# Block-diagonal queries times keys laid 64 per block of 32 queries, in a fused windowed-attention and feed-forward kernel

## The chip, the cores and the metric

The kernel runs on one NeuronCore of a Trainium2 chip. Its five engines are named here as in the profile: PE is TensorE (matrix products; PEld its weight loads), DVE is VectorE, ACT is ScalarE, POOL is GpSimd, and SP is SyncE, which here issues the DMAs. The metric is the time of one execution on the device, in microseconds (us); lower is better. A run before and after the change is compared by medians.

## What is computed

The reference is attention with fixed windows, followed by a normalised two-layer feed-forward with a residual. Cut to what matters:

```python
B, H, S, D = 8, 8, 576, 64
window, dilation = 32, 4
scores = q @ k.T / 8                      # per batch and head
rel = pos[:, None] - pos[None, :]
plain = (rel >= 0) & (rel < 32)                         # heads 0 to 3
dil   = (rel >= 0) & (rel < 128) & (rel % 4 == 0)       # heads 4 to 7
attn = softmax(where(mask, scores, -1e9))
x = (attn @ v), heads side by side        # (8, 576, 512)
xn = (x - mean) / sqrt(var + 1e-6) * g
out = x + relu(xn @ w_ch1) @ w_ch2        # 512 -> 2048 -> 512
```

Each query has at most 32 keys. In a plain head these are the last 32 positions; in a dilated head they are every fourth of the last 128. The host orders the dilated heads' positions by residue modulo 4 within each tile of 128, so that in both kinds of head a block of 32 queries needs just two blocks of 32 keys: its own and one before it, 64 scores a query.

## The kernel before

The 4608 rows are cut into 36 tiles of 128 positions, nine to each pair of sequences of 576, and the tiles into 12 blocks of three. A tile goes through loading (`load_tile_now`), preparation (`attn_prep`), scores, softmax (`attn_softmax`), values (`attn_values`), normalisation (`norm`) and a transposing DMA; a block then goes through the feed-forward (`ffn`: 16 up products' groups at L490, then down products at L513). All products are made in half precision from operands split into a high and a low half, with three products for each (high x high, low x high, high x low). The low half of an up product's result, `hl`, is made on VectorE at L497 from PSUM; the PSUM buffer `ps_z` comes free after it. There are two such buffers.

The weights come as 64-bit floats. During the first part of the run, chunk by chunk (32 of them), they are loaded into `w_raw` (five buffers, `RAWS`), brought to float32 by ScalarE (L548, L550), VectorE (L552, L553), TensorE (sums, L560) and GpSimd (L569), and split into halves (`split`, L141 to L149).

Queries and keys are prepared in two layouts. The first five tiles (`PACKED`) hold the plain heads in the lower 64 partitions and the dilated ones in the upper 64 (`prep_packed`); `Q_DVE` puts the queries' low half on VectorE in tiles 1 and 4 instead of on GpSimd. From tile 5 on (`prep_stacked`) queries stand with their high half in the lower partitions and their low half in the upper ones (L268, L269), and keys are loaded twice, once for each half of the partitions (L172, L173); tile 5 itself also rebuilds the keys of tile 4 in the new layout (L280, L281). The last 32 keys of the tile before are copied in front by GpSimd (L245).

Scores are made in two ways as well. In the first five tiles (`attn_scores_apart`) each block of 32 queries has products of its own, 64 rows by 32 columns of TensorE, and the scores come out compact: two mask additions of 128x256 on VectorE (L352). From tile 5 on (`attn_scores`) a head's 128 queries are multiplied by 160 keys (plain) or by 128 keys of this tile and 128 of the one before (dilated), and VectorE picks from PSUM, with the mask added, what each block of 32 queries needs: four additions of 32 partitions x 256 for the plain heads (L311) and four for the dilated ones (L325). Both kinds go through one PSUM tile, `ps_s`, of two banks.

The order of the work is written out: each step is a unit with a time, either by rules (pace, gaps) or, for most steps of the first tiles, from the table `TIMES`; units are emitted in order of these times, and a scheduler with a model of the engines orders the instructions of each engine from there, with L496 and L497 at high priority. Each engine then works in its order and waits on semaphores.

Of the kernel before, what the change touches and what calls it, by code (L numbers as in the profile page):

```python
# [7 lines left out]
F16 = mybir.dt.float16  # L8
# [8 lines left out]
P = 128  # L17
H = 8
# [12 lines left out]
NQK = 2 * HP * P  # L31
NBLK = NT // NB
PACKED = 5
EARLY = 5
# [8 lines left out]
Q_DVE = (1, 4, 5)  # L43
CW, RAWS = 1, 5
# [3 lines left out]
TAIL_POOL = 1  # L48
# [4 lines left out]
# Steps of the start that the rules of the plan would place elsewhere, and where they go.  # L53
# [3 lines left out]
# Powers of two that the norms of the scaled operands stay under: of the columns of w1 and w2 (L1),  # L57
# and of v (L2).
# [6 lines left out]
def attention_then_ffn(ctx: ExitStack, tc, qkv, masks, g, w1, w2, out):  # L65
# [23 lines left out]
    vh_b = [const.tile([P, H, D + 1], F16, name=f"vh{i}") for i in range(NV)]  # L89
    for i in range(NPT):  # L90
        nc.gpsimd.memset(pt_a[i], 0.0)
        nc.gpsimd.memset(pt_d[i], 0.0)
# [5 lines left out]
    # A quarter of w1's columns is at its number as halves (high, low), and before that one further as  # L98
    # float32; the last place then is free.
# [8 lines left out]
    # Chunk f is at f as halves (high, low), and before that as float32 four further, the last four  # L108
    # in the last place of w1.
# [55 lines left out]
    def load_tile_now(t):  # L165
        qk32 = work.tile([P, 2, 2, HP, P], F32, name="qk32", bufs=1)
        v32 = work.tile([P, H, D], F32, name="v32", bufs=1)
        if t < PACKED:
            nc.sync.dma_start(out=qk32[:, 0], in_=qkv[t, :, 0:NQK])
        else:  # L170
            src = qkv[t, :, 0:NQK].rearrange("(a d) e -> d a e", a=2)
            for on in (slice(0, D), slice(D, P)):  # L172
                nc.sync.dma_start(out=qk32[on].rearrange("d a x h c -> d a (x h c)"), in_=src)  # L173
        state["load", t] = nc.sync.dma_start(out=v32, in_=qkv[t, :, NQK:]).ins
        state[t] = dict(q32=qk32[:, :, 0], k32=qk32[:, :, 1], v32=v32)
# [29 lines left out]
    def stack_v(t):  # L205
        """The last values that plain heads of the next tile use, for products with (high, high, low)."""
# [6 lines left out]
    def rescale_v(t):  # L213
        """Brings tile t's values, split, to the scale of the next tile's, which is no larger."""
# [7 lines left out]
    def attn_prep(t):  # L222
        st = state[t]
        if t < PACKED:
            prep_packed(t)
        else:
            prep_stacked(t)
# [8 lines left out]
    def halves_of(x32, hi, lo, on_dve=False):  # L236
        nc.scalar.copy(hi, x32)  # L237
        (nc.vector if on_dve else nc.gpsimd).tensor_tensor(out=lo, in0=x32, in1=hi, op=ALU.subtract)  # L238

    def keys_before(t, old, new):  # L240
        """The last keys of the tile before."""
        if t % TPP == 0:
            nc.gpsimd.memset(new[:, :, 0:W], 0.0)
        else:
            (nc.gpsimd if TAIL_POOL else nc.vector).tensor_copy(new[:, :, 0:W], old[:, :, P : P + W])  # L245

    def prep_packed(t):
        """The first half of the heads in the lower half of the partitions, the second in the upper."""
# [542 lines left out]
```

## Time and profile before

| | us |
|---|---|
| median of three runs | 1007.41 |
| lowest and highest run | 1006.25, 1008.2 |
| span of the profiled execution, first to last instruction | 1002.2 |
| median less span: what lies around the instructions | 5.2 |
| busy in the span: TensorE, VectorE, GpSimd, ScalarE | 905.7, 666.6, 386.7, 336.9 |
| mean granted TensorE clock, as a share of full speed | 0.985 |

The profile comes from an execution of its own, and its span leaves out what precedes the first instruction and follows the last; the table puts the median beside it. A row of the groups' view names the line, the engine, the operation, what is written and read, the shapes and the count; then come the total busy time, the mean in nanoseconds, and the idle time of the engine just before, with what ended it. A row of the timeline begins with start and length in microseconds, and in brackets stands the idle time ahead of it and its releaser. A matmul's length includes its way through the array, so several are in flight at a time and only differences of starts tell what one costs in a row of them.

### The profile page before, as it was taken

What the parts mean: (1) busy time and instruction counts of PE and PEld (TensorE: products, weight loads), DVE (VectorE), ACT (ScalarE), POOL (GpSimd) and SP (SyncE); (2) the same over time, 40 slices, a digit from 0 to 9 for tenths busy, and PEclk for the clock granted to TensorE, in tenths of its full rate; (3) what the DMA queues carried; (4) which work ended last, traced back from release to release, by engine and by line L of the source; (5) the groups of instructions that cost most, each with busy time, mean ns of one, the idle gap of its engine ahead of it and who ended that gap; (6) DMA issues with size and microseconds to landing.
All of it is one profiled execution on the core that took longest, in us unless ns stands there. A gap on an engine that the chain in (4) does not pass through costs nothing.

```text
span 1002.2 us, 18434 instructions
## 1 busy us (share of the span) xinstructions
PE 905.7 (90%) x7396; PEld 537.7 (54%) x7396; DVE 666.6 (67%) x1458; ACT 336.9 (34%) x601; POOL 386.7 (39%) x371
## 2 busy tenths in 40 slices
PE   3255789999999989999999989999999999999998
PEld 2244765554555545555555545555555555565553
DVE  6999997694567476576667576586676576576111
ACT  6775673341222342233222242233232232221110
POOL 6777776361332342343342342343342342311000
PEclk9996899999999999999999999999999999999999
DMA  7565845333323553334423542343423333101000
GB/s 250 172 211 173 224 129 131 85 73 72 95 54 78 137 107 76 88 64 76 99 54 77 139 107 66 94 68 76 100 53 77 87 65 78 44 12 27 27 1 32
DMA packets 76742, 92.13 MB, mean 92 GB/s; under 512 B 48240, under 2 KB 50416, under 8 KB 76656
## 3 DMA queue, kind: packets, MB, share of 16 engines
q1 hardware_dynamic: 76656, 90.95, 37.9%
q8 instruction: 58, 0.95, 0.4%
q14 instruction: 28, 0.23, 0.1%
HBM read 70.45 MB, written 9.44 MB: 80 GB/s over the span
## 4 chain that ended last, share of the span: by engine, by line
PE 54%; DVE 24%; POOL 8%; DMA 5%; issue 4%; ACT 4%; SPq 1%; POOLq 0%; ACTq 0%; DVEq 0%
PE ps_o L513 27%; PE ps_z L490 20%; DVE pt_d L382 5%; PE ps_v L424 4%; DMA qk<-in_qkv 4%; POOL qs L269 3%; PE ps_s L293 2%; DVE hl L497 2%; DVE pt_a L376 2%; DVE w_sb L553 2%; DVE pt_a L378 2%; DVE sc L311 2%; DVE xn L456 1%; POOL sc L364 1%; POOL pk L371 1%
## 5 line engine op out<-in xcount | busy, mean ns | idle before, releaser
L513 PE MATMUL ps_o<-w_sb,hh 128*128 128x512 f16 x1152 | 339.3, 380 | 3.1 <-DVE w_sb L149 1.7
L490 PEld LDWEIGHTS <-w_sb 128*128 128x128 f16 x2688 | 241.2, 100 | 159.6 <-issue 17.2
L490 PE MATMUL ps_z<-xT,w_sb 128*128 128x384 f16 (+1 forms) x1536 | 211.6, 293 | 12.6 <-DVE hl L497 12.5
L490 PE MATMUL ps_z<-w_sb 128*128 128x384 f16 x1152 | 202.7, 326 | 9.4 <-DVE hl L497 9.3
L513 PE MATMUL ps_o<-w_sb,hl 128*128 128x512 f16 x576 | 210.8, 380 | 0.0
L497 DVE SCALAR_TENSOR_TENSOR hl<-ps_z,hh 128x384 f16<-128x384 f32 (+1 forms) x188 | 105.2, 562 | 110.8 <-ACT hh L496 107.9
L513 PEld LDWEIGHTS <-hh 128*128 128x128 f16 x1152 | 110.9, 98 | 125.3 <-issue 3.0
L496 ACT ACTIVATE hh<-ps_z 128x384 f16<-128x384 f32 (+1 forms) x188 | 92.2, 493 | 245.0 <-PE ps_z L490 244.9
L382 DVE STREAM_TRANSPOSE pt_d<-pk 32x256 f32<-32x256 f32 x144 | 90.9, 631 | 2.5
L238 POOL TENSOR_TENSOR kld<-qk,khd 128x512 f16<-128x512 f32 x31 | 35.9, 1158 | 141.4 <-ACT khd L237 140.0
L513 PEld LDWEIGHTS <-hl 128*128 128x128 f16 x576 | 56.5, 98 | 62.2 <-issue 2.5
L447 POOL TENSOR_TENSOR rstd<-rstd,mhalf 128x1 f32<-128x1 f32 x36 | 21.2, 589 | 170.6 <-DVE rstd L446 169.2
L269 POOL TENSOR_TENSOR qs<-qk,qs 64x1024 f16<-64x1024 f32 x31 | 66.0, 2129 | 32.4 <-ACT qs L268 30.6
L293 PEld LDWEIGHTS <-qs 64*32 64x32 f16 (+1 forms) x1464 | 60.9, 98 | 27.3 <-ACT khp L237 6.2
L311 DVE TENSOR_TENSOR sc<-ps_s,mask_sb 32x256 f32<-32x256 f32 x124 | 52.0, 419 | 29.9 <-PE ps_s L293 28.4
L238 POOL TENSOR_TENSOR klp<-qk,khp 128x512 f16<-128x512 f32 x36 | 42.9, 1193 | 69.8 <-ACT khp L237 61.2
L519 DVE SCALAR_TENSOR_TENSOR row<-ps_o,s,x 128x512 f32<-128x512 f32 x36 | 26.9, 749 | 62.1 <-PE ps_o L513 61.2
L462 POOL TENSOR_TENSOR xl<-xn,xh 128x512 f16<-128x512 f32 x36 | 43.1, 1198 | 43.2 <-ACT xh L461 43.1
L569 POOL TENSOR_TENSOR w_sb<-w_sb,w_raw 128x512 f32<-128x512 f32 x32 | 47.9, 1511 | 27.9 <-PE ps_o L560 12.5
L325 DVE TENSOR_TENSOR sc<-ps_s,mask_sb 32x256 f32<-32x256 f32 x124 | 52.0, 419 | 6.1 <-PE ps_s L293 4.2
L424 PE MATMUL ps_v<-vh,pt_a 128*128 128x65 f16 x288 | 38.5, 202 | 17.8 <-DVE pt_a L378 17.3
L148 ACT ACTIVATE vh<-v,sv 128x512 f16<-128x512 f32 x34 | 24.5, 721 | 89.5 <-PE ps_v L424 72.7
(97 smaller groups left out, 1100.6 us busy)
## 6 DMA issues: line engine op xcount, KB each, us to landing
qk<-in_qkv SPq DMA_DIRECT2D x67, 512.0 KB, 6.6
w_raw<-in_w SPq DMA_DIRECT2D x32, 512.0 KB, 4.7
v<-in_qkv SPq DMA_DIRECT2D x36, 256.0 KB, 3.0
out_x<-row SPq DMA_DIRECT2D x36, 256.0 KB, 2.0
row<-in_qkv SPq DMA_DIRECT2D x34, 256.0 KB, 3.6
v_b<-vh SPq DMA_DIRECT2D x64, 16.2 KB, 1.8
v_b<-vl SPq DMA_DIRECT2D x32, 16.0 KB, 2.0
xT<-xh SPq DMA_TRANSPOSE x18, 5.2
```

What stands on the lines that cost most here:

```text
L238: (nc.vector if on_dve else nc.gpsimd).tensor_tensor(out=lo, in0=x32, in1=hi, op=ALU.subtract)
L269: nc.gpsimd.tensor_tensor(out=qsv[D:P], in0=st["q32"][D:P], in1=qsv[D:P], op=ALU.subtract)
L293: nc.tensor.matmul(out, lhs, rhs, start=(n == 0), stop=(n == len(terms) - 1))
L311: nc.vector.tensor_tensor(out=sc[pj, 0:HP, :], in0=ps[pj, :, W * j : W * j + 2 * W], in1=mask_sb[pj, m : m + 1, :].broadcast_to([W, HP, 2 ...
L325: nc.vector.tensor_tensor(out=sc[pj, HP:H, :].rearrange("p h (t i) -> p h t i", t=2), in0=ps[pj].rearrange("p h (t c) -> p h t c", t=2)[:, ...
L382: nc.vector.transpose(dd[pj].rearrange("p t h (i r) -> p r t h i", r=DIL)[:, j], pk[pj, HP:H, :].rearrange("p h (t i) -> p t h i", t=2),)
L424: nc.tensor.matmul(oo, l, r, start=(n == 0), stop=(n == len(mm) - 1))
L490: nc.tensor.matmul(z[:, n], l, r, start=(m == 0), stop=(m == len(mm) - 1))
L496: nc.scalar.activation(hh, z, AF.Relu)
L497: nc.vector.scalar_tensor_tensor(out=hl, in0=z, scalar=0.0, in1=hh, op0=ALU.max, op1=ALU.subtract)
L513: nc.tensor.matmul(o, l, r, start=(f == 0 and m == 0), stop=(f == NFC - 1 and m == 2))
L569: nc.gpsimd.tensor_tensor(out=dst, in0=dst, in1=hi, op=ALU.mult)
```

## The change

There is one layout and one way of making scores for all tiles. The queries' tiles `q_b` (high and low, two of each) are cleared once and hold, for each half of a tile and each head, a 128x128 stationary operand: the lower 64 partitions have the dimensions of the first 32 queries, the upper 64 those of the next 32, each at its own columns, and the rest stays zero. The keys are laid beside it as 64 columns: in the lower partitions the 64 keys of the first block of queries, in the upper partitions those of the second. One product thus gives two blocks of compact scores, and two products (for the two halves of the tile) fill the 128 rows. The plain heads' keys are placed by the loads, with the last 32 keys of the tile before read again from memory; the dilated heads' keys of the tile before are copied on VectorE from its `kd`.

The scores of all heads fill one PSUM bank (`ps_s` has two buffers of one bank each now). They are masked in one addition of 128x512, or in two of 128x256 where plain and dilated heads need different masks (first, fifth and sixth tile of nine). In the softmax the separate float32 tile `p32` is gone: the high half is written first and the exponentials then replace the scores, of which there is one buffer instead of two. The raw weights have four buffers instead of five. `PACKED`, `EARLY`, `Q_DVE` and `TAIL_POOL` are gone; `TIMES` is as it was.

```diff
-CW, RAWS = 1, 5
+CW, RAWS = 1, 4
...
-    ps_s = ctx.enter_context(tc.tile_pool(name="ps_s", bufs=1, space=PSUM))
+    ps_s = ctx.enter_context(tc.tile_pool(name="ps_s", bufs=2, space=PSUM))
...
+    NQB = 2
+    q_b = [[const.tile([P, 2 * QPITCH], F16, name=f"q_{x}{i}") for x in "hl"] for i in range(NQB)]
+    for x in (x for pair in q_b for x in pair):
+        nc.gpsimd.memset(x.bitcast(F32), 0.0)
...
     def load_tile_now(t):
-        qk32 = work.tile([P, 2, 2, HP, P], F32, name="qk32", bufs=1)
+        q32 = work.tile([P, H, P], F32, name="q32", bufs=1)
+        k32 = work.tile([P, H * P + W], F32, name="k32", bufs=1)
         v32 = work.tile([P, H, D], F32, name="v32", bufs=1)
...
+        if t % TPP:
+            old = qkv[t - 1, 0:D, HP * P : NQK].rearrange("d (h c) -> d h c", h=HP)
+            nc.sync.dma_start(out=kv[lo, 0:HP, 0:W], in_=old[:, :, 3 * W : P])
+        nc.sync.dma_start(out=kv[lo, 0:HP, W:P], in_=keys[:, :, 0 : 3 * W])
+        nc.sync.dma_start(out=k32[lo, HP * P + W :], in_=qkv[t, D:P, HP * P : NQK])
+        nc.sync.dma_start(out=k32[hi, 0 : H * P].rearrange("d (a e) -> d a e", a=2), in_=src[1])
+        for on in (lo, hi):
+            nc.sync.dma_start(out=q32[on].rearrange("d (a h) c -> d a (h c)", a=2), in_=src[0])
...
+    def prep_qk(t):
+        st = state[t]
+        qh, ql = q_b[t % NQB]
+        q32 = st["q32"].rearrange("p h (b c) -> p b h c", b=2)
+        for a in range(2):
+            on, cols = slice(D * a, D * (a + 1)), slice(W * a, W * (a + 1))
...
+            nc.scalar.copy(at[0][:, :, :, cols], q32[on, :, :, cols])
+            nc.gpsimd.tensor_tensor(
+                out=at[1][:, :, :, cols], in0=q32[on, :, :, cols], in1=at[0][:, :, :, cols], op=ALU.subtract
+            )
+        kp = work.tile([P, 2, HP, P], F16, name="kp")
+        kd = work.tile([P, 2, HP, 2, 2, W], F16, name="kd", bufs=2)
...
+            nc.vector.tensor_copy(
+                kd[:, :, :, :, 0].rearrange("p x h b i -> p (x h) b i"),
+                state[t - 1]["kd"][:, :, :, :, 1].rearrange("p x h b i -> p (x h) b i"),
+            )
+        for (hi, lo), src in (
+            ((kp[:, 0], kp[:, 1]), k32[:, 0:HP]),
+            ((kd[:, 0, :, :, 1], kd[:, 1, :, :, 1]), k32[:, HP:H].rearrange("p h (b c) -> p h b c", b=2)[:, :, :, W:]),
+        ):
+            nc.scalar.copy(hi, src)
+            nc.gpsimd.tensor_tensor(out=lo, in0=src, in1=hi, op=ALU.subtract)
...
     def attn_scores(t):
...
+        ps = ps_s.tile([P, H, 2 * W], F32, name="ps_s")
+        for h in range(H):
+            mm = [(x[:, (b * H + h) * P : (b * H + h + 1) * P], y[2 * h + b]) for b in range(2) for x, y in st["terms"]]
+            for n, (l, r) in enumerate(mm):
+                nc.tensor.matmul(ps[:, h], l, r, start=(n == 0), stop=(n == len(mm) - 1))
+        sc = work.tile([P, H, 2 * W], F32, name="sc", bufs=1)
+        plain, dil = {0: 1, 4: 2}.get(tp, 0), {0: 3, 4: 4, 5: 5}.get(tp, 0)
+        for hs, m in ((slice(0, H), 0),) if plain == dil else ((slice(0, HP), plain), (slice(HP, H), dil)):
             nc.vector.tensor_tensor(
-                out=sc[pj, 0:HP, :],
-                in0=ps[pj, :, W * j : W * j + 2 * W],
...
+                out=sc[:, hs], in0=ps[:, hs],
+                in1=mask_sb[:, m : m + 1, :].broadcast_to([P, hs.stop - hs.start, 2 * W]), op=ALU.add,
             )
...
-        p32 = work.tile([P, H, 2 * W], F32, name="p32", bufs=1)
...
-        nc.scalar.activation(p32, sm, AF.Exp, scale=sc_qk)
         nc.scalar.activation(pk16[:, :, :, 0], sm, AF.Exp, scale=sc_qk)
-        nc.gpsimd.tensor_tensor(out=pk16[:, :, :, 1], in0=p32, in1=pk16[:, :, :, 0], op=ALU.subtract)
+        nc.scalar.activation(sm, sm, AF.Exp, scale=sc_qk)
+        nc.gpsimd.tensor_tensor(out=pk16[:, :, :, 1], in0=sm, in1=pk16[:, :, :, 0], op=ALU.subtract)
```

More of the change, by code (lines that the diff above doesn't have):

```diff
@@ L301, in attn_scores @@
+        st["terms"] = ((qh, kw[0]), (ql, kw[0]), (qh, kw[1]))
     def attn_scores(t):
@@ L303, in attn_scores @@
         tp = t % TPP
-        sc = work.tile([P, H, 2 * W], F32, name="sc")
-        ps = ps_s.tile([P, HP, 256], F32, name="ps_s")
-        for h in range(HP):
-            products(ps[:, h, 0 : W + P], [(x[:, h], y[:, h]) for x, y in st["plain"]])
-        m = {0: 1, 4: 2}.get(tp, 0)
-        for j in range(4):
-            pj = slice(W * j, W * (j + 1))
-            nc.vector.tensor_tensor(
-                out=sc[pj, 0:HP, :],
-                in0=ps[pj, :, W * j : W * j + 2 * W],
-                in1=mask_sb[pj, m : m + 1, :].broadcast_to([W, HP, 2 * W]),
-                op=ALU.add,
-            )
```

125 lines of the change are left out of this document (21 added, 104 removed).

## The prediction, made before the result was known

> **What bounds the kernel now.** I began with the page's head and its busy shares, then a table of three stretches by windows.
>
> ```profile
> span 1002.2 us, 18434 instructions
> PE 905.7 (90%) x7396; PEld 537.7 (54%) x7396; DVE 666.6 (67%) x1458; ACT 336.9 (34%) x601; POOL 386.7 (39%) x371
> ```
> ```profile
> 0.00:125.00 125.00, 59.73 (x1325) 52.24 (x1326) 113.58 (x217) 80.36 (x145) 89.56 (x85) 0.90 0.69 206
> 125.00:150.00 25.00, 22.71 (x239) 15.79 (x238) 24.06 (x50) 17.84 (x28) 18.16 (x13) 0.97 0.49 130
> 175.00:950.00 775.00, 753.12 (x5376) 431.69 (x5374) 502.54 (x1134) 223.94 (x406) 262.01 (x263) 1.00 0.35 76
> ```
>
> The columns are the stretch, its length, the busy time of PE, PEld, DVE, ACT and POOL, the granted clock, the DMA share and GB/s. Two kernels sit in one. In the first 125 us TensorE works 60 us, while VectorE works 114 and GpSimd 90: here the weights are converted and split, and VectorE sets the pace (24.06 of 25 us still in the next window). From 175 us on TensorE works 753 of 775 us: there a change is worth something only if it takes work from TensorE or ends one of its waits. So I asked next what TensorE waits for from 175 us to the end (microseconds in total, times, longest).
>
> ```profile
> PE ps_z L490 <- DVE hl L497: 15.9, 18, 1.5
> PE ps_v L424 <- DVE pt_a L378: 3.0, 6, 1.5
> ```
>
> Nearly all of it is VectorE being late with hl, the low half of an up product's result, which frees the PSUM buffer for the next product. 15.9 + 3.0 = 18.9 us is the most that a shorter VectorE queue can give back in that part. Then I looked at what stood in VectorE's queue ahead of a late hl; the timelines of both engines show it, here for the first and the last of five such places (at 372, 446, 598, 672 and 821 us).
>
> ```profile
> 370.00 1.72 DVE L311 TENSOR_TENSOR sc<-ps_s,mask_sb 32x256 f32<-32x256 f32 x4
> ...
> 818.28 1.72 DVE L311 TENSOR_TENSOR sc<-ps_s,mask_sb 32x256 f32<-32x256 f32 x4
> ```
> ```profile
> 372.36 0.32 PE L490 MATMUL ps_z<-w_sb 128*128 128x384 f16 x1 [1.48 <-DVE hl L497]
> ...
> 820.65 0.66 PE L490 MATMUL ps_z<-w_sb 128*128 128x384 f16 x3 [1.51 <-DVE hl L497]
> ```
>
> Four mask additions (L311), which the change removes, occupy VectorE for 1.72 us, and TensorE stands 1.5 us for the hl that had to queue behind them.
>
> **TensorE's own work.** The scores of a tile now take 48 products of 128x128 by 64 columns (8 heads, 2 halves of the tile, 3 terms), instead of 8 of 160 and 16 of 128 columns from tile 5 on, and instead of 144 of 64x32 in the first five tiles. A busy matmul time includes the pipeline, so I take starts.
>
> ```profile
> 401.82 0.19 PE L424 MATMUL ps_v<-vl,pt_d 128*128 128x64 f16 x1
> ...
> 402.09 0.19 PE L424 MATMUL ps_v<-vl,pt_d 128*128 128x64 f16 x1
> ...
> 408.41 0.23 PE L293 MATMUL ps_s<-khp,qs 128*128 128x160 f16 x1
> ...
> 408.96 0.59 PE L513 MATMUL ps_o<-w_sb,hh 128*128 128x512 f16 x2
> ...
> 414.47 0.22 PE L293 MATMUL ps_s<-khd,qs 128*128 128x128 f16 x1
> ...
> 415.36 3.74 PE L490 MATMUL ps_z<-xT,w_sb 128*128 128x384 f16 x22
> ```
> ```profile
> 109.82 0.23 PE L293 MATMUL ps_s<-khp,qs 64*32 64x64 f16 x6
> 109.88 0.19 PE L293 MATMUL ps_s<-klp,qs 64*32 64x64 f16 x3
> 109.90 0.23 PE L293 MATMUL ps_s<-khp,qs 64*32 64x64 f16 x6
> ```
>
> Products of the values have just the new shape: nine start in 402.09 - 401.82 = 0.27 us, 30 ns each. 48 of them are 1.44 us. The old ones: eight in 0.55 us and sixteen in 0.89, together 1.44. In the early tiles nine small ones start in 0.08 us, so 144 take 1.3 us. TensorE gains and loses nothing: the zero blocks of the queries cost no time, because the columns streamed stay about the same. The bound on the other side is the weight load, one per product.
>
> ```profile
> L293 PEld LDWEIGHTS <-qs 128*128 128x128 f16 x744 | 51.5, 98 | 15.6 <-DVE sc L311 1.4
> ```
>
> Were none of its 98 ns hidden, 48 - 24 = 24 more loads would cost 2.35 us a tile, 73 us over 31 tiles. I take zero, since the nine products above had a load each and started 30 ns apart. The Trainium skill, "TensorE: Matmul & The Clock Gate", section "LDWEIGHTS (loading the stationary operand)", gives a load columns / 1.2 ns, whatever the rows, some 107 ns here; paid in series that would add 24 x 107 ns x 31, an estimate of 80 us. By that rule the change fails; the trace agrees with the duration, 98 ns, and not with paying it in series.
>
> **VectorE and GpSimd, per tile.**
>
> ```profile
> L311 DVE TENSOR_TENSOR sc<-ps_s,mask_sb 32x256 f32<-32x256 f32 x124 | 52.0, 419 | 29.9 <-PE ps_s L293 28.4
> L325 DVE TENSOR_TENSOR sc<-ps_s,mask_sb 32x256 f32<-32x256 f32 x124 | 52.0, 419 | 6.1 <-PE ps_s L293 4.2
> ...
> L553 DVE SCALAR_TENSOR_TENSOR w_sb<-w_raw,w_sb 128x512 int32<-128x512 int32 x32 | 31.1, 985 | 0.2
> ...
> L433 DVE TENSOR_TENSOR x<-ps_v,rs 128x512 f32<-128x512 f32 x36 | 24.8, 688 | 0.8
> ...
> L552 DVE TENSOR_SCALAR w_sb<-w_sb 128x512 int32<-128x512 int32 x32 | 22.6, 719 | 1.8 <-ACT w_sb L548 1.4
> ...
> L352 DVE TENSOR_TENSOR sc<-ps_s,mask_sb 128x256 f32<-128x256 f32 x10 | 3.7, 410 | 0.0
> ...
> L238 DVE TENSOR_TENSOR qs<-qk,qs 128x512 f16<-128x512 f32 x2 | 2.5, 1227 | 0.0
> ...
> L281 DVE COPY kld<-klp 64x512 f16<-64x512 f16 x2 | 0.8, 388 | 0.1
> ```
> ```profile
> L269 POOL TENSOR_TENSOR qs<-qk,qs 64x1024 f16<-64x1024 f32 x31 | 66.0, 2129 | 32.4 <-ACT qs L268 30.6
> ...
> L238 POOL TENSOR_TENSOR kld<-qk,khd 128x512 f16<-128x512 f32 x31 | 35.9, 1158 | 141.4 <-ACT khd L237 140.0
> ...
> L245 POOL COPY khp<-khp 128x128 f16<-128x128 f16 x31 | 11.6, 374 | 11.5 <-PE ps_s L293 11.2
> ...
> L92 POOL MEMSET pt_d<- 128x1024 f32 x1 | 1.0, 955 | 0.0
> ```
>
> From tile 5 on eight additions of 419 ns (3.35 us) become one of 128x512 out of PSUM, for which L433 is the nearest row, 0.69; three tiles in nine need two masks, two of 0.41. Added is a VectorE copy of the old keys of the dilated heads (512 halves, nearest row L281, 0.39). Net 3.35 - 0.69 - 0.39 = 2.3 us less a tile. Two waits are new on VectorE, with hl queued behind them: the key copy waits for GpSimd's low keys of the tile before, and the additions for GpSimd's last pass over the same scores buffer, now a single one. Both end a tile earlier, so I cost them at nothing; where tiles crowd together, one GpSimd pass, 1.16, is the other end. GpSimd: the queries' low half is two of 64x512, half of L269 each, 2.13 together as before; the keys' second half shrinks from 1.16 to 0.58, and two copies of some 0.37 go: 1.3 us less. In the first five tiles it is the other way: q low was one 128x512 of 1.16 and becomes 2.13, and 0.58 is added for the dilated keys. Tiles 1 and 4 had q low on VectorE (L238, 1.23 each), which moves to GpSimd. For tiles 1 to 4 GpSimd thus gets 2 x 0.97 + 2 x 2.13 + 4 x 0.58 - 8 x 0.37 = 5.5 us more. It also clears the four query tiles once: 1088 words each, by the row below some 4 x 1.0 us, over before the conversions that VectorE begins at 9.27 us (a row further down), so I cost it at nothing, and at its 4 us if that cover fails. ScalarE gets about the same work, and at 80 of 125 us it has room.
>
> **Stretch to 125 us.** The first tile's load is six DMAs in SP's queue instead of two, ahead of the weights.
>
> ```profile
> 1.20 0.42 SPq L169 DMA_DIRECT2D qk<-in_qkv  x1
> ...
> 2.61 2.44 SPq L544 DMA_DIRECT2D w_raw<-in_w  x5
> ```
> ```profile
> 9.27 0.43 DVE L552 TENSOR_SCALAR w_sb<-w_sb 128x512 int32<-128x512 int32 x1 [1.40 <-ACT w_sb L548]
> 9.73 0.69 DVE L553 SCALAR_TENSOR_TENSOR w_sb<-w_raw,w_sb 128x512 int32<-128x512 int32 x1
> ```
> ```profile
> ACT w_sb L548 <- DMA w_raw<-in_w: 12.4, 9, 3.1
> ```
>
> Four more issues at 0.42 to 0.49 are 1.9 us, and VectorE's conversions, which wait for the first weights until 9.27, shift by it. Tiles 0 to 4 load 1 MB of queries and keys instead of 0.5: at the window's 206 GB/s 2.5 us of transfer each, and only four instead of five raw weight buffers run ahead. Queued behind these loads on SP are the weight loads, and ScalarE waits for those 12.4 us already, so nothing to 5 x 2.5 = 12.5 comes to light; I take 2.5, as VectorE's backlog covers most. GpSimd slows VectorE: alone L552 takes 0.43 and L553 0.69, on average 0.72 and 0.98; 32 x (0.29 + 0.29) = 18.6 us for GpSimd's 89.6, 0.21 each, so 5.5 us more cost 1.2. On VectorE itself: -2.5 (q low), +1.6 (four key copies; if each first waits out a GpSimd subtraction of 1.16, 6.2), -0.4 (additions of tiles 1 to 3, 0.82 to 0.69). Sum: 1.9 + 2.5 + 1.2 - 1.3 = +4.3. The Trainium skill, "SBUF — State Buffer", section "SBUF: two separate sides", says that VectorE (two SBUF inputs, or a two-port mode) and GpSimd hold a shared port pair in turn for a whole instruction; taken fully, those 5.5 us would cost 5.5, and the total be 4.3 us higher. L552's stretched mean agrees in kind, but 0.21 in size argues for 1.2.
>
> **Stretch 125 to 175 us.** Tile 5's eight additions become two (-2.5), its special transition from one key layout to the other goes (the two copies of 388 ns alone -0.8, smaller ones uncosted), one key copy comes (+0.4), and GpSimd has 1.3 us less in each of three tiles. VectorE is full there, so I count -2.9 in full and half of GpSimd's 3.9: -4.8.
>
> **From 175 us on.** At the five places 1.72 us of additions become 0.69: 5 x 1.03 = 5.2. Of the other 9 us of waiting for hl, most behind transposes that stay, I take a third, 3, since all of VectorE's queue is 2.3 us shorter a tile. -8.2, between 0 (the waits form again behind the transposes) and -18.9.
>
> Sum: 4.3 - 4.8 - 8.2 = -8.7. The profiled span is 1002.2; the median of the three runs is 1007.41, 5.2 more for what lies around the span, and that stays. 1007.4 - 8.7 = 998.7.
>
> **Rivals.** *The start loses more than the rest gains.* The weights become late: the five larger loads show in full (12.5 instead of 2.5) and each key copy waits out a subtraction (6.2 instead of 1.6), so the first stretch costs 18.9, against 13.0 gained later: +5.9, 1013.3. It decides from a start that loses over 13.0 us. For it: ScalarE's 12.4 us. Against: VectorE is busy 114 of 125, so loads are seldom the last to come. *Waits form anew:* hl waits behind transposes instead, the start's terms cancel: 1007. *More than forecast:* most of the 18.9 goes and the start is neutral: 1007.4 - 15 - 4.8 = 987.6. *Weight loads in series:* +73 - 8.7, 1072; the 30 ns speak against it.
>
> **The numbers.** Forecast 0.50 (its own range 992 to 1005), more than forecast 0.15, no change 0.10, slow start 0.22, loads in series 0.03. About 0.2%, 2 us, is what a measurement of this kernel can tell. Faster 0.65, same 0.10, slower 0.25; the range 986 to 1015 leaves out the loads in series and the tails of both sides.
>
> **What would show it.** L311 and L325 gone, one or two additions near 0.69 in all a tile; score products 30 ns apart; TensorE's wait for hl from 175 us on down from 15.9 to some 8; the first conversion near 11 us and the last weight's conversion some 4 us later than now. Wrong if the score products start over 50 ns apart, if the hl waits stay near 16, or if the last conversion comes over 13 us later.

## The result, and the profile after

The changed kernel takes 1031.01 us, the median of four runs (1028.36 to 1033.89), beside 1006.87 for the kernel before (four runs): a ratio of 1.0236, 95% interval 1.0214 to 1.0258, or 24.1 us more. The forecast was 998.7, its range ended at 1015, and slower had a chance of 0.25. The direction was wrong, and the size lies outside the range.

The head of the page after, with the busy shares, and then the windows that the prediction read (stretch, length, busy time of PE, PEld, DVE, ACT and POOL with instructions, granted clock, DMA share, GB/s):

```profile
span 1032.1 us, 19046 instructions
PE 912.2 (88%) x7660; PEld 543.6 (53%) x7660; DVE 596.6 (58%) x1270; ACT 348.9 (34%) x642; POOL 374.7 (36%) x356
```
```profile
0.00:125.00 125.00, 46.66 (x593) 40.81 (x594) 107.84 (x193) 74.43 (x133) 92.71 (x85) 0.89 0.67 196
125.00:150.00 25.00, 22.06 (x410) 21.39 (x408) 23.04 (x46) 16.40 (x31) 18.21 (x17) 0.93 0.77 186
175.00:950.00 775.00, 746.95 (x6074) 430.49 (x6074) 429.17 (x968) 230.32 (x431) 244.32 (x242) 0.99 0.32 78
```

VectorE has 70 us less to do over the span, as forecast, and the kernel is slower all the same. In the first 125 us TensorE did 47 us of work instead of 60: the start is behind. To see by how much, both spans are cut at the first, the sixth and the last store of an output tile. First the kernel before, then the changed one, in the columns as above:

```profile
0.00:165.30 165.30, 96.54 (x1662) 75.41 (x1663) 148.30 (x293) 105.70 (x182) 120.34 (x105) 0.91 0.63 184
165.30:262.70 97.40, 92.17 (x714) 53.94 (x713) 63.71 (x142) 26.38 (x45) 35.99 (x38) 1.00 0.40 89
262.70:999.30 736.60, 716.95 (x5025) 408.40 (x5022) 454.56 (x1023) 204.84 (x374) 230.39 (x229) 1.00 0.33 72
```
```profile
0.00:190.00 190.00, 99.54 (x1221) 79.21 (x1221) 163.20 (x294) 112.61 (x196) 136.05 (x116) 0.89 0.65 181
190.00:291.30 101.30, 96.13 (x810) 55.45 (x810) 50.45 (x110) 28.65 (x51) 32.42 (x34) 0.97 0.30 75
291.30:1029.30 738.00, 716.51 (x5635) 408.90 (x5633) 382.98 (x866) 207.63 (x395) 206.22 (x207) 1.00 0.29 71
```

To the first output 24.7 us are lost, to the sixth 3.9 more, and in the 737 us behind it 1.4. That is 30.0, the difference of the two profiled spans (29.9); the profiled execution of the changed kernel was its longest run, hence more than the 24.1 of the medians. From the sixth output on VectorE does 454.6 - 383.0 = 71.6 us less, and TensorE's busy time and the length of the stretch stay as they were.

What TensorE waited for from 175 us to the end (microseconds, times, longest):

```profile
PE ps_v L373 <- DVE pt_a L327: 13.9, 16, 2.3
PE ps_z L439 <- DVE hl L446: 10.9, 13, 1.7
```

The waits for hl went from 15.9 to 10.9, and those of the value products (L373) for transposed probabilities from 3.0 to 13.9. The gain was made and given back.

**The conversions of the weights**, which pace the start. The first, then the last of the changed kernel, then the last of the kernel before, from VectorE's timelines:

```profile
12.78 0.43 DVE L501 TENSOR_SCALAR w_sb<-w_sb 128x512 int32<-128x512 int32 x1 [1.18 <-ACT w_sb L497]
...
145.18 0.67 DVE L502 SCALAR_TENSOR_TENSOR w_sb<-w_raw,w_sb 128x512 int32<-128x512 int32 x1
```
```profile
121.69 1.18 DVE L553 SCALAR_TENSOR_TENSOR w_sb<-w_raw,w_sb 128x512 int32<-128x512 int32 x1
```

The first comes 3.5 us later (9.27 before), the last 23.5 us. The prediction had named over 13 as the point at which it is wrong. The groups on VectorE up to the first output show one thing that fills the time; before, then after (busy, mean ns):

```profile
L553 DVE SCALAR_TENSOR_TENSOR w_sb<-w_raw,w_sb 128x512 int32<-128x512 int32 x32 | 31.1, 985 | 0.2
...
L149 DVE SCALAR_TENSOR_TENSOR vl<-v,sv,vh 128x512 f16<-128x512 f32 x5 | 4.7, 941 | 0.0
```
```profile
L502 DVE SCALAR_TENSOR_TENSOR w_sb<-w_raw,w_sb 128x512 int32<-128x512 int32 x32 | 35.7, 1115 | 0.5
L501 DVE TENSOR_SCALAR w_sb<-w_sb 128x512 int32<-128x512 int32 x32 | 25.3, 791 | 3.4 <-ACT w_sb L497 3.0
...
L154 DVE SCALAR_TENSOR_TENSOR vl<-v,sv,vh 128x512 f16<-128x512 f32 x5 | 8.6, 1713 | 1.1 <-ACT vh L153 1.1
...
L271 DVE COPY kd<-kd 128x512 f16<-128x512 f16 x7 | 5.2, 742 | 7.8 <-POOL kd L280 7.8
```

The same instructions take longer: 32 conversions 35.7 us instead of 31.1, five subtractions of the values 8.6 instead of 4.7. (The 7.8 us ahead of the key copy lie before the first work of the span and hold nothing up.) I take for every operation on the same tiles and of one shape its shortest instance in the same trace as its undisturbed time, and the rest as stretched; what stretches it, the account doesn't say. To the first output, VectorE's time then is

| VectorE to the first output, us | before | after | difference |
|---|---|---|---|
| idle | 17.0 | 26.8 | 9.8 |
| undisturbed work | 122.7 | 125.4 | 2.7 |
| stretched | 25.6 | 37.8 | 12.2 |
| sum | 165.3 | 190.0 | 24.7 |

Counted to the end of the last conversion instead (122.9 and 145.9 us), idle time grows by 8.3 us, undisturbed work by 7.6 and stretch by 7.2: no one of the three is the loss by itself.

GpSimd is busy 120.3 and 136.1 us in these stretches. Its groups there, before and then after:

```profile
L238 POOL TENSOR_TENSOR klp<-qk,khp 128x512 f16<-128x512 f32 x8 | 10.6, 1322 | 0.2
...
L269 POOL TENSOR_TENSOR qs<-qk,qs 64x1024 f16<-64x1024 f32 x3 | 6.4, 2131 | 5.4 <-ACT qs L268 5.3
...
L238 POOL TENSOR_TENSOR qs<-qk,qs 128x512 f16<-128x512 f32 x3 | 3.5, 1157 | 4.9 <-ACT qs L237 4.9
```
```profile
L261 POOL TENSOR_TENSOR q_l<-q,q_h 64x512 f16<-64x512 f32 x16 | 21.7, 1358 | 1.9 <-ACT q_h L260 1.3
...
L94 POOL MEMSET q_h<- 128x1088 f32 x2 | 2.0, 1006 | 0.0
L94 POOL MEMSET q_l<- 128x1088 f32 x2 | 2.0, 1004 | 0.0
```

The queries' low halves take 21.7 us instead of 6.4 + 3.5 = 9.9, and the clearing of their tiles 4.0.

### The profile page after: what moved, and what is told of

It reads as the page before. It is cut to its first block, busy times and chain, and to the rows that moved or that the text cites. A ratio compares the mean times of both kernels' runs of the same rounds, so it can differ in the third digit from the quotient of the medians.

```text
span 1032.1 us, 19046 instructions
## 1 busy us (share of the span) xinstructions
PE 912.2 (88%) x7660; PEld 543.6 (53%) x7660; DVE 596.6 (58%) x1270; ACT 348.9 (34%) x642; POOL 374.7 (36%) x356
## 4 chain that ended last, share of the span: by engine, by line
PE 58%; DVE 16%; DMA 7%; POOL 6%; ACT 6%; issue 5%; SPq 2%; POOLq 0%; ACTq 0%
PE ps_o L462 29%; PE ps_z L439 22%; PE ps_v L373 5%; DVE pt_d L331 4%; DMA row<-in_qkv 3%; POOL q_l L261 3%; DVE pt_a L325 2%; PE ps_s L298 2%; DVE w_sb L502 2%; DMA q<-in_qkv 2%; DVE pt_a L327 2%; DMA k<-in_qkv 1%; POOL sc L314 1%; ACT q_h L260 1%; DVE w_sb L154 1%
## 5 line engine op out<-in xcount | busy, mean ns | idle before, releaser
L462 PE MATMUL ps_o<-w_sb,hl 128*128 128x512 f16 x576 | 213.6, 381 | 0.0
L261 POOL TENSOR_TENSOR q_l<-q,q_h 64x512 f16<-64x512 f32 x72 | 86.9, 1206 | 75.5 <-ACT q_h L260 71.1
L280 POOL TENSOR_TENSOR kp<-k,kp 128x512 f16<-128x512 f32 x36 | 42.3, 1174 | 97.7 <-ACT kp L279 97.6
L298 PEld LDWEIGHTS <-q_h 128*128 128x128 f16 x1152 | 62.2, 100 | 16.5 <-POOL q_l L261 9.4
L320 POOL TENSOR_TENSOR pk<-sc,pk 128x512 f16<-128x512 f32 x36 | 46.5, 1291 | 44.6 <-ACT sc L319 44.6
L411 POOL TENSOR_TENSOR xl<-xn,xh 128x512 f16<-128x512 f32 x36 | 45.3, 1260 | 42.7 <-ACT xh L410 42.7
L373 PE MATMUL ps_v<-vh,pt_a 128*128 128x65 f16 x288 | 38.6, 203 | 24.3 <-DVE pt_a L327 24.3
L298 PEld LDWEIGHTS <-q_l 128*128 128x128 f16 x576 | 53.3, 100 | 7.8 <-POOL q_l L261 1.8
L325 DVE STREAM_TRANSPOSE pt_a<-pk 32x128 f32<-32x128 f32 x144 | 43.5, 302 | 16.7 <-POOL pk L320 15.1
```

The source lines that it names most:

```text
L261: nc.gpsimd.tensor_tensor(out=at[1][:, :, :, cols], in0=q32[on, :, :, cols], in1=at[0][:, :, :, cols], op=ALU.subtract)
L298: nc.tensor.matmul(ps[:, h], l, r, start=(n == 0), stop=(n == len(mm) - 1))
L320: nc.gpsimd.tensor_tensor(out=pk16[:, :, :, 1], in0=sm, in1=pk16[:, :, :, 0], op=ALU.subtract)
L325: nc.vector.transpose(a[pj, :, W * j : W * (j + 1)], pk[pj, 0:HP, W : 2 * W])
L373: nc.tensor.matmul(oo, l, r, start=(n == 0), stop=(n == len(mm) - 1))
L411: nc.gpsimd.tensor_tensor(out=xl, in0=xn, in1=xh, op=ALU.subtract)
```

## The experiments

Eighteen kernels were run. The letters in the first expectations stand for these theories. The larger loads, and fewer buffers for the raw weights, hold the weights up (A). The written-out times of the first steps suit the old work and no other (B). From the sixth tile on the values' steps are due too early (C). GpSimd's added preparation stretches VectorE (D). All times below are differences to the kernel before, measured beside each (1005.8 to 1007.4 us); the changed kernel stands at +24.1.

### One part of the change alone, in the kernel before

**b_raws4**, four raw buffers:

```diff
-CW, RAWS = 1, 5
+CW, RAWS = 1, 4
```

> The kernel before with four raw weight buffers instead of five, nothing else changed. Theory A (the start is late because weight loads can run less far ahead and larger tile loads stand in front of them): 5 to 12 us slower than before, last weight conversion near 130 us instead of 121.7. Theory B (what is lost is the fit between the written-out order of the first steps and the work they now hold, not the buffers or loads): within 3 us of before.

1011.82: +5.4 (ratio 1.0051, 1.0029 to 1.0074). **b_wide**, 0.5 MB in four DMAs more for each of the first five tiles, read by nobody:

```diff
             nc.sync.dma_start(out=qk32[:, 0], in_=qkv[t, :, 0:NQK])
+            for x in range(2):
+                for on in (slice(0, D), slice(D, P)):
+                    nc.sync.dma_start(out=qk32[on, 1, x], in_=qkv[t, on, x * HP * P : (x + 1) * HP * P])
```

> The kernel before, with four more DMAs in each of the first five tiles that bring the same 0.5 MB of queries and keys a second time into the unused half of their tile; nothing reads them. Theory A: 5 to 10 us slower than before, first conversion near 11.5 us instead of 9.3. Theory B: the shift of the first load alone, at most 3 us slower.

1017.85: +11.5 (1.0110, 1.0073 to 1.0147). **b_three**, both of these (the four DMAs as above), and the queries' low half on GpSimd in tiles 1 and 4 too:

```diff
-Q_DVE = (1, 4, 5)
-CW, RAWS = 1, 5
+Q_DVE = ()
+CW, RAWS = 1, 4
```

> The kernel before with four raw buffers, the doubled loads of the first five tiles, and the low half of the queries on GpSimd in tiles 1 and 4 too. Theory A: most of the loss, 15 to 24 us slower than before. Theory B: under 8 us.

1014.71: +8.3 (1.0100, 1.0048 to 1.0152). Each of two small parts costs more than the 4.3 that I had given the whole start, and together they cost no more than the larger loads alone. The parts don't add up.

### Parts of the change taken back

**a_half**: tiles 1 to 4 load only the lower 64 partitions of keys and queries; what is computed from the upper ones is then of old data. The two tiles lie outside the rotating buffers for that.

```diff
-        q32 = work.tile([P, H, P], F32, name="q32", bufs=1)
-        k32 = work.tile([P, H * P + W], F32, name="k32", bufs=1)
+        q32, k32 = q32_c, k32_c
...
-        for on in (lo, hi):
+        if t not in (1, 2, 3, 4):
+            nc.sync.dma_start(out=k32[hi, 0 : H * P].rearrange("d (a e) -> d a e", a=2), in_=src[1])
+        for on in (lo, hi)[: 1 if t in (1, 2, 3, 4) else 2]:
```

> The changed kernel, with the loads of tiles 1 to 4 cut to the lower 64 partitions of queries and keys (0.5 MB in four DMAs, as many bytes as before the change); the upper half keeps tile 0's values, so this leaves out half of the loading of four tiles and computes with stale values there. Theory A (bytes and DMAs in front of the weight loads): 8 to 14 us faster than the changed kernel, 1017 to 1023. If the bytes matter little against the preparation on GpSimd: within 4 us of 1031.

1031.67: +25.5 (1.0260, 1.0204 to 1.0315), no gain in all. Its windows, to its first, sixth and last output:

```profile
0.00:194.30 194.30, 106.12 (x1397) 84.45 (x1398) 160.34 (x299) 115.91 (x202) 134.47 (x121) 0.93 0.62 171
194.30:280.50 86.20, 83.78 (x631) 46.56 (x628) 47.66 (x107) 24.79 (x44) 27.50 (x28) 1.00 0.34 81
280.50:1025.00 744.50, 721.02 (x5640) 410.48 (x5637) 385.49 (x866) 208.06 (x397) 206.39 (x207) 0.99 0.28 70
```

With half the bytes the first output comes no earlier (194.3 us), but the sixth comes at 280.5 instead of 291.3, and the stretch behind it is 6.5 us longer (744.5 instead of 738.0). Some of this can be the spread between executions (5.5 us among the four of the changed kernel). So the bytes are not cleared: the start gains as much as in a_noql below, and why it is lost again behind the sixth output is not shown.

**a_raws5** and **a_raws5_nqb1**: five raw buffers again. The room for the fifth comes from single buffers for `kp` and `xl` in the first, and from one pair of query tiles in the second.

```diff
-CW, RAWS = 1, 4
+CW, RAWS = 1, 5
...
-        kp = work.tile([P, 2, HP, P], F16, name="kp")
+        kp = work.tile([P, 2, HP, P], F16, name="kp", bufs=1)
...
-        xl = work.tile([P, DM], F16, name="xl")
+        xl = work.tile([P, DM], F16, name="xl", bufs=1)
```

> The changed kernel with five raw weight buffers; for room one buffer instead of two for the plain keys in half precision (kp) and for the low half of the normalised rows (xl). Theory A: 4 to 8 us faster than the changed kernel, as the kernel before lost 5.4 by the fourth buffer. If the single kp and xl buffers cost as much: within 3 us.

```diff
-CW, RAWS = 1, 4
+CW, RAWS = 1, 5
...
-    NQB = 2
+    NQB = 1
```

> The changed kernel with five raw weight buffers again; for room the block-diagonal queries have one pair of tiles instead of two. Theory A: 6 to 12 us faster than the changed kernel (1019 to 1025). Theory B: within 3 us of it (1028 to 1034).

1034.07 and 1024.72: +27.9 (1.0284, 1.0253 to 1.0315) and +18.3 (1.0179, 1.0142 to 1.0215). The last conversion ends at 136.1 and 132.4 us instead of 145.9. In the first kernel the sixth output comes at 280.3 us, but the stretch from there to the last takes 749.7 instead of 738.0, so nothing is gained at the end; I put that to the single buffers, which is not shown. In the second, with one pair, the queries of tile 6 are overwritten by those of tile 7 (at 163 us) before their products run (at 193 us): it computes something else, and its time is not that of the full work. This pair decides nothing about the fifth buffer alone.

**a_noql**: the queries' low subtraction on GpSimd left out in the first five tiles (the products read zeros there).

```diff
+            if t >= 5:
-            nc.gpsimd.tensor_tensor(
+              nc.gpsimd.tensor_tensor(
```

> The changed kernel without the two GpSimd subtractions for the low half of the queries in the first five tiles (that low half is left out there and reads as zero). Theory D (GpSimd's added preparation in the start, through the slowed VectorE): 2.1 us less GpSimd work in each of five tiles makes it 6 to 12 us faster than the changed kernel. Theory A alone: within 4 us of 1031.

1024.20: +18.0 (1.0185, 1.0139 to 1.0232), 6.1 less than the changed kernel. Its windows to its first, sixth and last output, and the two VectorE groups as above to its first output (its lines lie one further on from the edit):

```profile
0.00:193.50 193.50, 108.76 (x1384) 85.85 (x1385) 153.73 (x312) 118.19 (x205) 122.83 (x113) 0.81 0.66 178
193.50:281.50 88.00, 85.87 (x643) 47.78 (x642) 44.93 (x93) 23.05 (x42) 25.52 (x26) 0.98 0.35 85
281.50:1018.00 736.50, 715.51 (x5637) 408.54 (x5635) 383.59 (x866) 207.94 (x396) 206.53 (x207) 1.00 0.30 71
```
```profile
L503 DVE SCALAR_TENSOR_TENSOR w_sb<-w_raw,w_sb 128x512 int32<-128x512 int32 x32 | 30.6, 967 | 0.2
L502 DVE TENSOR_SCALAR w_sb<-w_sb 128x512 int32<-128x512 int32 x32 | 20.5, 646 | 5.4 <-ACT w_sb L498 5.2
...
L154 DVE SCALAR_TENSOR_TENSOR vl<-v,sv,vh 128x512 f16<-128x512 f32 x5 | 5.9, 1182 | 4.6 <-ACT vh L153 4.5
```

The conversions are at 30.6 us again, the values' subtractions at 5.9. VectorE's stretched time to the sixth output falls from 39.2 to 27.7, and the sixth output comes 9.8 us earlier (281.5). This is the one part of the work whose removal made the whole changed kernel faster. That it did so by removing the stretch is not shown: VectorE's idle time to the sixth output rises from 77.6 to 82.9, the last conversion ends at 151.3 us instead of 145.9 and the first output comes at 193.5 instead of 190.0; and in a_half, which keeps these subtractions, the sixth output is as early.

**h_raws4**: a mixture. The first five tiles keep the old form (their loads, their preparation, their products of 64x32); from tile 5 on all is as changed; four raw buffers.

```diff
+PACKED = 5
+Q_DVE = (1, 4)
...
-        prep_qk(t)
+        (prep_packed if t < PACKED else prep_qk)(t)
...
+        if t < PACKED:
+            return scores_apart(t)
```

> The changed kernel from tile 5 on, with the first five tiles as they were before: one load of 0.5 MB each, packed layout, products of 64 rows by 32 columns, low half of the queries on VectorE in tiles 1 and 4; four raw buffers, one scores buffer. Theory A: the start is that of the kernel before with four raw buffers, about 1012 in all. If instead the new work from tile 5 on or the single scores buffer makes the start late: over 1020.

1011.89: +5.6 (1.0055, 1.0015 to 1.0095). That is b_raws4 (+5.4) to within 0.2 us, with intervals of some 4 and 2 us: from tile 5 on the new form is worth nothing that can be seen. And it is 18.5 us below the changed kernel: that much of the loss lies in the form of the first five tiles, or in how that form fits the table of times, which is the same here. TensorE's waits in h_raws4 from 175 us on:

```profile
PE ps_v L434 <- DVE pt_a L388: 14.0, 16, 2.3
PE ps_z L500 <- DVE hl L507: 9.4, 10, 1.8
```

They are those of the changed kernel, so they belong to the new form from tile 5 on. In b_raws4 the same two are 3.8 and 10.6. VectorE's stretched time to the sixth output is 20.8 us in h_raws4 and 37.4 in b_raws4, yet they reach it at 271.8 and 274.5: the account of VectorE says where its time went, and not what would be gained without it. The 37.4 are also 8.1 more than in the kernel before (29.3), though b_raws4 gives GpSimd no preparation more.

**h_raws5** is the mixture with five raw buffers, for which `pk`, `xh` and `xl` have one buffer each.

```diff
-CW, RAWS = 1, 4
+CW, RAWS = 1, 5
...
-        pk = work.tile([P, H, 2 * W], F32, name="pk")
+        pk = work.tile([P, H, 2 * W], F32, name="pk", bufs=1)
```

> The kernel with the first five tiles as before the change and the new work from tile 5 on, with five raw weight buffers; for room one buffer instead of two for the probabilities (pk) and for both halves of the normalised rows (xh, xl). If four raw buffers are all that it still loses: 1005 to 1008, the kernel before. If the shorter VectorE queue from tile 5 on is worth anything: under 1003.

1017.72: +11.5 (1.0121, 1.0078 to 1.0164), no gain. No kernel that does all of the work beat the kernel before.

### The order

**b_times0** and **a_times0**: the table of written-out times emptied in both kernels, so that the rules place every step.

```diff
-TIMES = {'s0': 5.79, 'N4': 105.06,
...
+TIMES = {}
```

> The kernel before with an empty table of times. Theory B: it loses 15 to 25 us against 1007, which is what the table is worth where it fits. Theory A: it loses under 10 us.

> The changed kernel with an empty table of times for the first steps, so that the rules alone place them. To be read against the kernel before with the same empty table. Theory A (resources: tile loads, raw buffers): this pair is 15 to 24 us apart, as the unedited pair is. Theory B (the table fits the old work only): the pair is under 10 us apart, and this one no slower than the changed kernel with the table (1031).

1041.77 and 1044.64: +35.4 (1.0353, 1.0323 to 1.0383) and +38.3 (1.0382, 1.0352 to 1.0412). The table is worth 35.4 us to the kernel before and 14.2 to the changed one; without it the two are 2.9 us apart. That looked like theory B.

**a_v25**: values and transposing DMAs due 5 us later in a tile's plan. It acts from tile 9 on, as the table gives these times for all tiles before.

```diff
-SOFTMAX, VALUES, READY = 10.0, 20.0, 28.0
+SOFTMAX, VALUES, READY = 10.0, 25.0, 33.0
```

> The changed kernel with the values of a tile, and what follows them, placed 5 us later than the rule has it (25 instead of 20, 33 instead of 28). Theory C (from tile 6 on TensorE is sent to the values of a tile just before VectorE's transposes of it end, which is where the gain of the shorter VectorE queue went): its waits for the transposed probabilities fall from 14 to under 5 us and the time by 6 to 12 us. Rival: the waits only move back to hl, within 3 us of 1031.

1039.84: +33.5 (1.0334, 1.0281 to 1.0387). TensorE's waits for transposed probabilities from 175 us on fall only from 13.9 to 12.5 and those for hl from 10.9 to 10.6, and two waits for the transposing DMAs, 3.8 and 2.9, are new. Theory C falls for these tiles: later steps don't end the waits.

Then four kernels to part theory B from the theory of added work. **b_noql** does less, under the same table: the queries' low subtraction is left out in the first five tiles of the kernel before.

```diff
-        qh, ql = qs[:, 0:HP], qs[:, HP:H]
-        halves_of(st["q32"][:, 0], qh, ql, t in Q_DVE)
+        qh = ql = qs[:, 0:HP]
+        nc.scalar.copy(qh, st["q32"][:, 0])
```

> The kernel before with less to do in its first five tiles: the queries' low half isn't subtracted there (the products read the high half in its place), about 1.2 us of GpSimd work in three tiles and 1.2 us of VectorE work in two. Theory of added work (each microsecond of preparation in the first 125 us shows, about as in the changed kernel, where leaving out the same step gave 6.8 us): faster than before by 2 to 5 us, about 1002. Theory of the fitted order (the listed times suit the old work, and any other work under them loses): no faster than before, 1006 to 1012, though less is done.

**b0_wide**, **b0_raws4** and **a0_noql** are b_wide, b_raws4 and a_noql, each with its edit as above and the table empty.

```diff
-TIMES = {'s0': 5.79, 'N4': 105.06,
...
+TIMES = {}
```

> The kernel before with an empty table of times, and 0.5 MB in four DMAs more for each of the first five tiles. With the table these loads cost 11 us. Theory of added work: they cost the same without it, about 1052. Theory of the fitted order: they cost little without it, within 4 us of the 1041.8 of the kernel before with an empty table.

> The kernel before with an empty table of times and four raw weight buffers instead of five. With the table this costs 5.4 us. Theory of added work: about 1047. Theory of the fitted order: within 3 us of 1041.8.

> The changed kernel with an empty table of times and without the queries' low subtractions on GpSimd in the first five tiles (the products read zeros there). Theory of added work: about 7 us below the 1044.6 of the changed kernel with an empty table, 1038. Theory of the fitted order: with no written times there is nothing to fit, so only what GpSimd itself takes from VectorE, 10 us x 0.21 to 0.4, 2 to 4 us: 1041 to 1043.

b_noql is 1001.14: -4.7 (0.9946, 0.9927 to 0.9964), faster, where a table that suits only the old work should lose. Its VectorE is stretched more to the sixth output, 32.3 us instead of 29.3, so here the gain is not a gain of stretch. b0_wide is 1047.76 and b0_raws4 1048.00, +41.9 (1.0415, 1.0395 to 1.0435) and +42.2 (1.0411, 1.0379 to 1.0443): 6.5 and 6.8 more than b_times0. a0_noql is 1032.63, +26.8 (1.0258, 1.0230 to 1.0285): 11.5 less than a_times0, and in this pair the stretch to the sixth output falls with the time, from 40.4 to 24.9. The costs are there with and without the table:

| difference made by, us | with the table | without |
|---|---|---|
| queries' low subtractions left out, before | -4.7 | not run |
| the same, changed kernel | -6.1 | -11.5 |
| four raw buffers, before | 5.4 | 6.8 |
| larger loads, before | 11.5 | 6.5 |
| the whole change | 24.1 | 2.9 |

So theory B falls as the whole cause, and the last row still says that without the table the change as a whole costs little. The windows of b_times0 and then a_times0, to the first and the sixth output, show where it goes:

```profile
0.00:158.90 158.90, 91.86 (x1543) 68.83 (x1543) 142.47 (x261) 93.46 (x153) 110.60 (x97) 0.91 0.56 168
158.90:309.40 150.50, 116.40 (x915) 73.16 (x916) 93.94 (x224) 45.12 (x84) 59.85 (x60) 0.84 0.44 97
```
```profile
0.00:167.70 167.70, 85.54 (x1060) 67.54 (x1061) 134.36 (x240) 100.64 (x167) 116.68 (x103) 0.75 0.62 176
167.70:311.40 143.70, 120.29 (x1121) 75.77 (x1119) 91.21 (x205) 49.77 (x95) 62.65 (x61) 0.88 0.47 108
```

Even there the change is 8.8 us late at the first output. But without the table the next five outputs take 150.5 and 143.7 us, instead of 97.4 and 101.3 with it, and there 6.8 us are caught up. I read that as slack, of which the table leaves none; no run shows it directly.

**a_tlate** and **a_tearly** move the same work: the listed steps of tiles 1 to 5 come 8 us later or earlier.

```diff
+TIMES = {k: x + 8.0 * (k[0] in 'LASMVNT' and k[1:] in ('1', '2', '3', '4', '5')) for k, x in TIMES.items()}
```

> The changed kernel, with the listed times of the steps of tiles 1 to 5 (loads, preparation, scores, softmax, values, normalisation, transposes) 8 us later, so that the weights go ahead of them. Theory of added work: the same work in the same 125 us ends at about the same time, 1029 to 1034. Theory of the fitted order: the time moves by over 5 us, down to 1015 to 1025 if the tiles now come too early for the weights behind them, up if they feed TensorE too late.

> The changed kernel, with the listed times of the steps of tiles 1 to 5 8 us earlier, the mirror of the run before. Theory of added work: 1029 to 1034. Theory of the fitted order: the time moves by over 5 us, in the other direction than with 8 us later.

1043.37 and 1028.13: +36.0 (1.0374, 1.0333 to 1.0416) and +20.7 (1.0211, 1.0166 to 1.0257). Order alone, with all the work the same, is worth 15 us between the two, though 8 us either way found only 3.4 of gain, which the intervals don't tell from none. Any edit here also changes the order that the scheduler makes (in b_raws4 VectorE's order differs from that of the kernel before from its fourteenth instruction on), so a difference of a few us between two of these kernels is not the price of the edited part alone.

**What is settled and what is open.** Shown: the loss arises before the sixth output (windows); 18.5 of 24.1 us belong to the form of the first five tiles under this table (h_raws4), and four raw buffers cost 5 to 7 in the kernel before; of the five tiles' work, the queries' low halves on GpSimd cost 6 to 12 us. Not shown: that they cost it by stretching VectorE, for which a_noql and a0_noql speak and b_noql and b_raws4 don't. The old form pays 4.7 for the same, so this tells only for some 1.4 to 6.8 of the 18.5 (the upper end sets a difference without the table against one with it). Open: how the other 12 to 17 divide among the larger loads, their six issues, the key copies and the order. The clearing isn't among them, since the mixture clears the same tiles. Loads cost 11.5 when added to the old kernel; halved in the new one, they gave 10.8 by the sixth output and nothing at the end. That fits several limits near each other, of which the removal of one uncovers the next, but this is argued and not shown. The key copies were not tried by themselves. Nor was a table made for the new work, so what the change would cost under one is open: the 24.1 are its cost under a table made for the old work, the 2.9 its cost without any.

## Why the prediction was wrong

**TensorE neutral: right.** The score products of the changed kernel, from its timeline of TensorE:

```profile
603.63 0.19 PE L298 MATMUL ps_s<-kd,q_l 128*128 128x64 f16 x1
603.66 0.22 PE L298 MATMUL ps_s<-kd,q_h 128*128 128x64 f16 x2
603.72 0.19 PE L298 MATMUL ps_s<-kd,q_l 128*128 128x64 f16 x1
...
604.10 0.19 PE L298 MATMUL ps_s<-kd,q_h 128*128 128x64 f16 x1
```

Seventeen starts lie between 603.63 and 604.10, 29 ns apart as forecast (30), with a load each. The Trainium skill's load time ("TensorE: Matmul & The Clock Gate", "LDWEIGHTS (loading the stationary operand)") is thus hidden here, and the rival "loads in series" is out.

**VectorE less per tile: right.** L302 takes 0.68 us for 128x512 (0.69 forecast), and from the sixth output on VectorE has 71.6 us less to do over 30 tiles, 2.4 a tile (2.3 forecast).

**The stretch to 125 us, +4.3: the step that failed.** The last conversion came 23.5 us later instead of some 4, the first output 24.7. The term that the runs show too small is loads and buffers: put at 2.5, they cost 11.5 and 5.4 when each is added alone to the kernel before, and 8.3 together with the moved subtractions. The term for GpSimd, 1.2, may be too small as well: the queries' low halves alone cost 1.4 to 6.8 more than in the old form. How the rest of the 24.7 arises stays open. The terms:
- *First load*, 1.9: the first weights are issued at 5.71 instead of 2.61, since the six loads ahead of them take SP 0.59 to 0.76 us each to issue and the two of before took 0.42 and 0.43, and the first conversion is 3.5 late. Too small, by little.
- *Loads and buffers*, 2.5 of a bound of 12.5, "as VectorE's backlog covers most". In the kernel before, the loads alone cost 11.5 and four buffers 5.4. ScalarE's wait for the raw weights in the first 150 us rose from 12.4 to 17.5 us:

```profile
ACT w_sb L497 <- DMA w_raw<-in_w: 17.5, 12, 3.1
```

  The cover that the prediction counted on wasn't there: each part alone costs more than the 2.5. By which path it costs is open. VectorE's idle time to the first output grew by 9.8 us, but only 1.6 of them (3.0 instead of 1.4) ended with ScalarE's first step on the weights.
- *GpSimd slows VectorE*, "0.21 each, so 5.5 us more cost 1.2". GpSimd was busy 15.7 us more to the first output, not 5.5: 11.8 for the queries' low halves, 4.0 for the clearing that I "cost at nothing", 4.6 for the normalised rows of two more tiles that fell before it, less 5.0 for keys, and small ones. VectorE was stretched by 12.2, some 0.8 for each. The 0.21 was an average of two conversion forms over all of GpSimd's work. The other number that the prediction had from a page (the Trainium skill, "SBUF — State Buffer", "SBUF: two separate sides": one of the two holds the port pair for a whole instruction) would have been one for one. The 0.8 lies nearer to that. But no run shows a fixed price: in b_raws4 VectorE was stretched 6.9 us more to the first output for 2.3 more of GpSimd. In a_noql the whole kernel gained 6.1 us for 13.2 of GpSimd's time (136.05 to 122.83), half of one for one, and VectorE stood idle more.
- *VectorE itself*, -1.3: its undisturbed work to the first output grew by 2.7. The key copies, forecast at 0.39, take 0.28 alone and 0.74 in this stretch.

**125 to 175 us, -4.8: failed.** From the end of the last conversion to the first output it was 165.3 - 122.9 = 42.4 us before and 190.0 - 145.9 = 44.1 after.

**From 175 us on, -8.2: half right.** The hl waits fell by 5.0, but value products now wait 10.9 us more for transposes. Net the stretch from the sixth output on is 1.4 longer. This is what the rival "waits form anew" said of this part, though it expected hl itself to wait behind the transposes. Why the transposes come later in the new form is not settled. (The bound of 18.9 left out 2.1 us in which TensorE waited for VectorE's other transposes, `pt_d`; nothing rests on it.)

**The rival that came nearest** was the slow start, whose condition, a start that loses over 13.0 us, was met with 24.7. Its price of 18.9 less 13.0 of later gain was too low on both counts: the start lost more, and nothing was gained later.

## What to carry to other kernels

Price a change separately for each stretch. If the order of the work is written out for the old form, count the misfit of the new form as a cost of its own, and try the change once without the written order. In one where an engine is busy 90% of the time in a fixed order, count late loads, fewer buffers and a neighbour's added work at their upper bounds until a row shows what covers them. Work taken off an engine that isn't the bound is worth only the waits that it ends, and these can form again at the next step of the same chain. Before changing layouts, try the new form only where the old one is slow: the mixture showed here at once which tiles carried the loss.

## What was unexpected of the hardware

How much VectorE is slowed beside GpSimd differs widely by instruction. The key copy, half precision in and out of SBUF (shortest, median and longest time in ns, over the whole span):

```profile
L271 DVE COPY kd<-kd x32: 279/694/1244, 7.8 to 887.4; 128x512 f16<-128x512 f16 x32
```

It takes 279 ns at the least and up to 4.5 times that. The four copies beside which GpSimd ran nothing took 279 to 294 ns, and all 22 that took over 600 ns had GpSimd busy beside them for at least nine tenths of their time. The other six took 280 to 286 ns with GpSimd busy beside them for most of it, so running side by side is not enough by itself. The mask additions out of PSUM (L302, 128x256) take 406 to 426 ns over the whole span, with GpSimd busy beside them or not. A mean from one group, such as the 0.21 us for each of GpSimd's taken from the conversions, doesn't carry over to others.
